# Small score pieces of two groups in one tile: windowed attention beside linear attention on one core

## The chip, the cores and the metric

The kernel runs on one core of a Trainium2 chip. That core has a matrix engine (PE in the profile, with its weight loads shown as PEld), a vector engine (DVE), a scalar engine (ACT), a general engine (POOL) and an engine that issues DMAs (SP). They run side by side and wait for each other through semaphores. The metric is the device time of one execution in microseconds (us), as a median of runs.

## The reference

Two attention blocks, A and B, each have an input of 2048 tokens x 640, weights of 640 x 1920 for queries, keys and values, and an output matrix of 640 x 640. There are 32 heads of 20 numbers each. The outputs of the two stand side by side.

```python
# A: sliding window of 256 keys
scores = jnp.einsum("bhqd,bhkd->bhqk", q, k) * (Dh ** -0.5)
mask = (idx[:, None] - idx[None, :] >= 0) & (idx[:, None] - idx[None, :] < W)
p = _softmax(jnp.where(mask[None, None], scores, -1e9), axis=-1)
o = jnp.einsum("bhqk,bhkd->bhqd", p, v)
return (lambda x, *d: x.transpose(*d))(o, 0, 2, 1, 3).reshape(B, S, D) @ wo
# B: linear attention
phi = lambda t: jnp.where(t > 0, t + 1, jnp.exp(t)) + 1e-6
kv = jnp.einsum("bhsd,bhse->bhde", phi(k), v)
den = jnp.einsum("bhqd,bhd->bhq", phi(q), z)[..., None] + 1e-6   # z: sum of phi(k)
o = jnp.einsum("bhqd,bhde->bhqe", phi(q), kv) / den
```

## The kernel before

**Segments, groups, pairs.** Tokens are cut into four segments of 512 (`SB`), s = 0 to 3. Heads are cut into eight groups of four (`NG`); groups are taken in pairs, g and h = g + 1. The four heads of a group lie in the four 32-row strips of PE's array, so that four matmuls with a depth of 20 can run beside each other.

**Pieces and tiles of scores.** For a segment and a group, the scores of the window are cut into pieces: blocks of 128 keys against a run of 64 to 256 queries (`first`, `before`, `last`), and a "middle" of four pieces of 64 queries (`M`). In a middle piece the upper 64 rows of the array's output are 64 keys of one block and the lower 64 rows are keys of the block two back, so that every one of its matmuls has 64 weight columns: the profile writes these 20*64, and the others 20*128. A tile holds 512 columns for each of four heads: it fills four PSUM banks, and there is one such tile in PSUM (`S_ps`), so a tile's scores can begin when the exponential of the tile before has read its own. `tiles_of` (L39) lists the tiles: for a pair in segment 0 four tiles, and else five, 76 in all.

**What happens to a tile.** `scores` (L752) writes the matmuls (L762), then one exponential on ACT over the whole tile (L780), which writes the tile `p` in SBUF, and then POOL sets to zero what lies outside the window, with `affine_select` (L794). A select of kind D or E (the diagonal and the window's far edge) works on 128 columns of each head, in place. A middle has two selects of 256 columns of each head: the first copies into a tile of its own, `plow`, what the own block keeps, and the second works in place on `p` for the far block.

**Values.** When a group has all its tiles, `values` (L805) is due two units later (`LAG = 2`): its matmuls (L821, 128*32: 128 keys, 32 output rows for each head) run over the group's pieces in the order of its tiles, four heads for each piece, 40 matmuls in segment 0 and 56 in the others. They read `p`, or `plow` for a middle's own block. DVE then transposes the result and divides it.

**The order.** A loop over the 76 tiles (from L1082) writes one unit for each: the scores of a tile, then the values of a group that is due, then as much filling work as the unit has credit for (`take`, L1067). Filling work is all else that PE does: projections of both blocks, the sums and outputs of B, the output projections. It comes from a plan with times (`plan`), in an order written ahead; every engine carries out its own instructions in that order. Filling work in the main loop evacuates PSUM with ACT or DVE, whichever has less load by the kernel's own account (`evac`).

**The start.** The first 512 tokens of A's x are loaded as they lie, in two halves (L172), and turned on PE (`transposes`, L178, with copies on DVE and ACT, L184 and L186). The weights of v come in two parts (L948), the first with `K0` of five blocks of 128 rows. `v_abreast` (L437) runs four chains of v's products beside each other in four PSUM banks: first all products whose weights are in the first part, then, chain by chain, the rest, with an evacuation after each. Then the second half of x is turned, and the other four chains of v follow. The weights of q and k are regrouped on three engines (L350 to L356), and their first chains precede the loop.

Of the kernel before, what the change touches and what calls it, by code (L numbers as in the profile page):

```python
# [9 lines left out]
P = 128  # L10
# [3 lines left out]
BF16 = mybir.dt.bfloat16  # L14
# [6 lines left out]
SB = 512  # L21
TPS = SB // P
# [10 lines left out]


HALF = P // 2
LOW = 2 * P


def tiles_of(s):  # L39

    def first(g):
        return [(g, 0, 64, 256, 0, P), (g, 1, 192, 256, HALF, P)], [("D", 0, P), ("E", SB - P, P)]

    def before(g, c):
        return [(g, -1, 0, 192, c, HALF), (g, -2, 0, 64, c + 192, HALF)], [("E", c + P, P)]

    def last(g, c):
        return [(g, 3, 448, 64, c, HALF), (g, 2, 320, 192, c + 64, HALF)], [("D", c, P)]

    def middle(g):  # L60
        return [(g, "M", P * i, HALF, LOW + HALF * i, HALF) for i in range(TPS)], [("M", LOW, LOW)]

    def tile_of(done, *pieces):
        return s, sum((p for p, _ in pieces), []), sum((q for _, q in pieces), []), done

    out = []
    for g in range(0, NG, 2):
        h = g + 1
        if s == 0:
            for gi in (g, h):  # L70
                out += [tile_of(None, first(gi)), tile_of(gi, last(gi, 0), middle(gi))]
            continue
        out += [
            tile_of(None, first(g)),
            tile_of(None, before(g, 0), middle(g)),
            tile_of(g, last(g, 0), middle(h)),
            tile_of(None, first(h)),
            tile_of(h, before(h, 0), last(h, 2 * P)),
        ]
    return out  # L80

# [11 lines left out]
def kernel(  # L93
# [11 lines left out]
    _, S, D = A_x.shape  # L105
# [9 lines left out]
    def pool(name, bufs, space=None):  # L115
        if space is None:
            return ctx.enter_context(tc.tile_pool(name=name, bufs=bufs))
        return ctx.enter_context(tc.tile_pool(name=name, bufs=bufs, space=space))
# [6 lines left out]
    pp = pool("p", 5)  # L125
    pqp = pool("pq", 2)
    op1 = pool("o1", 2)
    pl_ = pool("plow", 2)
    np_ = pool("norm", 1)
    tp = pool("turned", 1)  # L130
    rp = pool("rows", 2)
# [33 lines left out]
    def load_x_first():  # L165

        tok = pqp.tile([P, TPS, D], BF16, name="phi")
        src = xsrc["A"][0:SB, :].rearrange("(t p) d -> p t d", p=P)
        t = xp.tile([P, KT, SB], BF16, name="xA")

        def load(i):
            nc.sync.dma_start(out=tok[:, 2 * i : 2 * i + 2, :], in_=src[:, 2 * i : 2 * i + 2, :])  # L172

        def transposes(i):
            for tb in (2 * i, 2 * i + 1):
                ps = dps.tile([P, 2 * SB], BF16, name="dense")
                for c in range(KT):
                    nc.tensor.transpose(  # L178
                        ps[:, c * P : (c + 1) * P], tok[:, tb, c * P : (c + 1) * P], ident[:]
                    )  # L180
                dst = t[:, :, tb * P : (tb + 1) * P]
                pv = ps[:, 0:D].rearrange("p (c q) -> p c q", q=P)
                if tb % 2:
                    nc.scalar.activation(out=dst, in_=pv, func=ACT.Copy)  # L184
                else:
                    nc.vector.tensor_copy(out=dst, in_=pv)  # L186

        return t, load, transposes
# [67 lines left out]
    def evac(dst, src, n=SB, to=None):  # L256

        if to is None:
            to = "A" if load["A"] < load["D"] + AHEAD else "D"
        load[to] += n + COPY  # L260
        if to == "A":
            nc.scalar.activation(out=dst, in_=src, func=ACT.Copy)
        else:
            nc.vector.tensor_copy(out=dst, in_=src)

    def bank(wide=False):
        flush(begun[0] - 2)
        begun[0] += 1
        settle(False)
        if wide:  # L270
            return dps.tile([P, 2 * SB], BF16, name="dense")
        return dps.tile([P, SB], F32, name="dense")
# [40 lines left out]
    xA, xB = {}, {}  # L313
    q_pad, k_pad, v_tok = {}, {}, {}
# [6 lines left out]
    pieces = []  # L321
    for c in range(KT):
        m = EXTRA * c
        while m < EXTRA * (c + 1):
            n = min(EXTRA * (c + 1) - m, DH - m % DH)
# [83 lines left out]
    by_tokens = [(tb, i) for tb in range(TPS) for i in range(2)]  # L409
# [10 lines left out]
    def v_rows(ps, dst, tb, i):  # L420
        evac(
            dst[:, tb, i * hh : (i + 1) * hh, 0:DH],
            ps[:, 0 : hh * DH].rearrange("p (h d) -> p h d", d=DH),
            hh * DH,
        )
# [11 lines left out]
    def v_abreast(xt, dst, order, k0):  # L437
        pss = [bank() for _ in order]
        for ps, (tb, i) in zip(pss, order):
            for kt in range(k0):  # L440
                v_product(ps, xt, tb, i, kt)
        for ps, (tb, i) in zip(pss, order):
            for kt in range(k0, KT):
                v_product(ps, xt, tb, i, kt)
            v_rows(ps, dst, tb, i)

# [303 lines left out]
    def scores(s, parts, selects):  # L752
        S_ps = sps.tile([P, 4, SB], F32, name="S_ps")
        p_all = pp.tile([P, 4 * SB + 2], BF16, name="p")
        p = p_all[:, 0 : 4 * SB].rearrange("p (j q) -> p j q", j=4)
        nc.scalar.activation(out=p_all[0:1, 4 * SB : 4 * SB + 1], in_=ident[0:1, 0:1], func=ACT.Copy)

        def product(g, kb, k0, k1, q0, n, col, step):
            kt = k_pad[kb // TPS]
            ko = (kb % TPS) * P  # L760
            for j in range(4):
                nc.tensor.matmul(  # L762
                    columns(S_ps[k0:k1], j, col, n, step),
                    lhsT=kt[32 * j : 32 * j + DH, g, ko + k0 : ko + k1],
                    rhs=q_pad[s][32 * j : 32 * j + DH, g, q0 : q0 + n],
                    start=True,
                    stop=True,
                    tile_position=(32 * j, k0),
                )

        for g, rel, q0, n, col, step in parts:
            if rel == "M":
                own = key(s, q0 // P)
                product(g, own, 0, HALF, q0, n, col, step)

                far = own - 2 if own >= 2 else own
                product(g, far, HALF, P, q0 + (HALF if own >= 2 else 0), n, col, step)
            else:
                product(g, key(s, rel), 0, P, q0, n, col, step)
        nc.scalar.activation(out=p, in_=S_ps[:], func=ACT.Exp, scale=scale)  # L780
        add_load(a=2080)
        low = None
        if any(kind == "M" for kind, _, _ in selects):
            low = pl_.tile([P, 4, LOW], BF16, name="plow")
        for kind, c0, n in selects:

            v = p[:, :, c0 : c0 + n].rearrange("p j (b q) -> p j b q", q=HALF)
            if kind == "M":
                lv = low[:, :, c0 - LOW : c0 - LOW + n].rearrange("p j (b q) -> p j b q", q=HALF)
                jobs = [(lv, v, 1, 0), (v, v, -1, -HALF - 1)]  # L790
            else:
                jobs = [(v, v, 1, HALF) if kind == "D" else (v, v, -1, -1)]
            for dst, src, sgn, base in jobs:
                nc.gpsimd.affine_select(  # L794
                    out=dst,
                    in_=src,
                    pattern=[[0, 4], [0, n // HALF], [sgn, HALF]],
                    compare_op=ALU.is_ge,
                    fill=0.0,
                    base=base,  # L800
                    channel_multiplier=-sgn,
                )
        return p, low

    def values(s, g, held):  # L805
# [3 lines left out]
        todo = []  # L809
        for (_, rel, q0, n, col, step), (p, low) in held:  # L810
            if rel == "M":
                own = key(s, q0 // P)
                todo.append((own, low, q0, n, col - LOW, step))
                if own >= 2:
                    todo.append((own - 2, p, q0 + HALF, n, col, step))
            else:
                todo.append((key(s, rel), p, q0, n, col, step))
# [123 lines left out]

    xA[0], load_half, transposes = load_x_first()

    K0 = 2
    wv = A_wqkv.rearrange("(kt p) n -> p kt n", p=P)
    load_half(0)
    for k0, k1 in ((0, K0), (K0, KT)):
        nc.sync.dma_start(out=w_sb["A"][:, k0:k1, :], in_=wv[:, k0:k1, 2 * D : 3 * D])  # L948
# [4 lines left out]
    xB[0] = load_x("B", 0)  # L953
    dummies = warm_up((28, 3))
    next(dummies)
    transposes(0)
    next(dummies)
    v_tok[0] = v_bufs[0]
    v_abreast(xA[0], v_tok[0], by_tokens[0:4], K0)
    transposes(1)  # L960
    a_v0 = v_proj(xA[0], v_tok[0], by_tokens[4:])
    run(banks(a_v0, 2))
    regroup(0, raw[0], dve_copy, in_turn(act_copy, pool_copy))
# [118 lines left out]
    for i, (s, parts, selects, done) in enumerate(units):  # L1082
        p = scores(s, parts, selects)
# [6 lines left out]
        if ready and ready[0][0] + LAG <= i:  # L1090
            last = i == len(units) - 1
            if last:
                credit -= take(2000)
            _, at = ready.popleft()
# [10 lines left out]
    while ready:  # L1105
        take(5500)
        _, at = ready.popleft()
# [36 lines left out]
```

## Time and profile before

| what | before |
|---|---|
| median of 3 runs | 261.02 us (260.02 to 261.86) |
| profiled execution, its own time | 261.33 us |
| span of the profiled execution | 259.6 us |
| PE busy | 247.7 us, 95% |
| ACT, DVE, POOL busy | 200.3, 177.0, 171.8 us |
| exponentials of tiles (L780) | 76, 1.87 us each |
| selects of 512 elements, of 1024 into `p`, of 1024 into `plow` (L794) | 120, 32, 32; 0.71, 1.26, 1.21 us each |
| granted PE clock | 1.00 |

The span runs from the first to the last instruction of one execution; the time beside it is the device's own for the same execution. A row of the profile names a line, an engine, an operation, what it writes and reads, and the shape. "Busy" of PE is modelled: matmuls overlap, so a row's busy time is a union and not a sum of lengths. In a timeline, a row has its start and its length in us, and xN says that N instructions of one kind were drawn together; in square brackets are the idle time of the engine ahead of it and what ended it.

### The profile page before, as it was taken

The numbers are of one execution on the slowest core, as the hardware profiler recorded it, in microseconds if no ns is written. First come the engines' busy times: TensorE is split into PE (matmuls) and PEld (weight loads), VectorE is DVE, ScalarE is ACT, GpSimd is POOL, SyncE is SP. The second block draws the span as 40 slices with busy tenths as digits, with TensorE's granted clock in tenths as the row PEclk, the third lists the DMA queues.
The fourth block names the chain that finished last, engine by engine and source line by source line (L and its number), as shares of the span: only waits on it lengthen the run. The fifth ranks groups of instructions, "written<-read, shape, count | busy, mean of one in ns | idle before, by whom it ended". The sixth has DMA issues, their size and how long they took to land.

```text
span 259.6 us, 10761 instructions
## 1 busy us (share of the span) xinstructions
PE 247.7 (95%) x4722; PEld 142.4 (55%) x4769; DVE 177.0 (68%) x308; ACT 200.3 (77%) x260; POOL 171.8 (66%) x211
## 2 busy tenths in 40 slices
PE   8699999999999999999999999999999999999995
PEld 7444445556445745555456555555456554555573
DVE  0245686786745456866655578599889879978662
ACT  3376887899776788988676788888879998988742
POOL 6113777777696766759485796949767594976800
PEclk9999999999999999999999999999999999999999
DMA  6996579699568993502484591622857286975725
GB/s 186 312 231 182 79 198 136 103 279 216 92 95 247 114 257 88 163 3 48 84 132 122 58 190 43 170 43 59 173 89 174 48 188 168 109 136 120 233 47 186
DMA packets 65012, 36.35 MB, mean 140 GB/s; under 512 B 48197, under 2 KB 63941, under 8 KB 64965
## 3 DMA queue, kind: packets, MB, share of 16 engines
q1 hardware_dynamic: 64965, 35.67, 64.6%
q8 instruction: 37, 0.61, 1.0%
q14 instruction: 10, 0.08, 0.1%
HBM read 14.42 MB, written 9.83 MB: 93 GB/s over the span
## 4 chain that ended last, share of the span: by engine, by line
PE 80%; POOL 6%; issue 4%; ACT 3%; DVE 3%; DMA 3%; SPq 0%; ACTq 0%; DVEq 0%
PE dense L277 43%; PE S_ps L762 10%; PE dense L545 9%; PE dense L821 8%; PE dense L412 7%; POOL p L794 4%; DMA wA<-in_A_wqkv_dram 3%; ACT p L780 2%; POOL plow L794 2%; PE dense L652 1%; PE dense L695 1%; DVE phi L294 1%; ACT e L287 1%; PE dense L624 1%; DVE e L291 1%
## 5 line engine op out<-in xcount | busy, mean ns | idle before, releaser
L780 ACT ACTIVATE p<-S_ps 128x2048 bf16<-128x2048 f32 x76 | 142.4, 1873 | 33.9 <-PE S_ps L762 33.1
L794 POOL TENSOR_SCALAR_AFFINE_SELECT p<-p 128x512 bf16<-128x512 bf16 (+1 forms) x152 | 123.3, 822 | 63.8 <-ACT p L780 58.5
L277 PE MATMUL dense<-xA,wqk 128*128 128x512 bf16 x183 | 47.2, 379 | 1.1 <-issue 0.6
L794 POOL TENSOR_SCALAR_AFFINE_SELECT plow<-p 128x1024 bf16<-128x1024 bf16 x32 | 38.8, 1211 | 2.2
L762 PE MATMUL S_ps<-qpad,kpad 20*64 20x64 bf16 (+3 forms) x1728 | 35.2, 213 | 0.4
L762 PEld LDWEIGHTS <-kpad 20*64 20x64 bf16 (+1 forms) x1728 | 17.4, 100 | 30.0 <-issue 25.5
L834 DVE STREAM_TRANSPOSE T<-dense 128x512 f32<-128x512 f32 x32 | 22.8, 712 | 12.6 <-PE dense L821 12.5
L277 PEld LDWEIGHTS <-wqk 128*128 128x128 bf16 x200 | 18.5, 98 | 20.6 <-issue 1.3
L412 PE MATMUL dense<-wA,xA 128*128 128x320 bf16 x160 | 27.7, 300 | 2.1 <-DMA wA<-in_A_wqkv_dram 1.8
L291 DVE TENSOR_SCALAR e<-e 128x512 bf16<-128x512 bf16 x40 | 22.0, 550 | 10.7 <-ACT e L287 10.1
L294 DVE SCALAR_TENSOR_TENSOR phi<-dense,e 128x512 bf16<-128x512 f32 x40 | 27.7, 692 | 1.5
L821 PE MATMUL dense<-p,vA 128*32 128x64 bf16 (+2 forms) x1152 | 27.1, 223 | 0.5 <-POOL p L794 0.5
L277 PE MATMUL dense<-wB,xB 128*128 128x128 bf16 (+1 forms) x156 | 25.4, 297 | 0.8 <-issue 0.6
L287 ACT ACTIVATE e<-dense 128x512 bf16<-128x512 f32 x40 | 23.4, 594 | 2.5 <-PE dense L277 2.2
L277 PE MATMUL dense<-wo,oT 128*128 128x128 bf16 (+2 forms) x154 | 24.3, 296 | 1.0 <-issue 0.6
L545 PE MATMUL dense<-phi,tok 128*128 128x128 bf16 (+1 forms) x154 | 24.3, 296 | 0.7 <-issue 0.3
L277 PE MATMUL dense<-xB,wB 128*128 128x512 bf16 x90 | 24.2, 380 | 0.6 <-issue 0.3
L821 PEld LDWEIGHTS <-vA 128*32 128x32 bf16 x1664 | 22.2, 96 | 3.5 <-issue 1.4
L277 PE MATMUL dense<-wB,xA 128*128 128x512 bf16 (+1 forms) x156 | 23.4, 297 | 0.5 <-issue 0.3
L851 DVE TENSOR_TENSOR N<-T,recA 128x320 bf16<-128x320 f32 (+1 forms) x28 | 18.7, 668 | 3.1 <-DMA oT<-N 2.2
L412 PEld LDWEIGHTS <-xA 128*128 128x128 bf16 x160 | 14.3, 98 | 11.2 <-issue 3.1
L731 DVE TENSOR_TENSOR tok<-tok,rden 128x640 bf16<-128x640 bf16 x16 | 19.8, 1238 | 0.0
(68 smaller groups left out, 237.7 us busy)
## 6 DMA issues: line engine op xcount, KB each, us to landing
out_dram<-osb SPq DMA_DIRECT2D x7, 640.0 KB
x_scr<-xB SPq DMA_DIRECT2D x4, 640.0 KB
tok<-in_B_x_dram SPq DMA_DIRECT2D x4, 640.0 KB
xB<-x_scr SPq DMA_DIRECT2D x4, 640.0 KB
wB<-in_B_wqkv_dram SPq DMA_DIRECT2D x3, 800.0 KB
q_scr<-qpad SPq DMA_DIRECT2D x16, 60.0 KB
k_scr<-kpad SPq DMA_DIRECT2D x16, 60.0 KB
qpad<-q_scr SPq DMA_DIRECT2D x16, 60.0 KB
```

The lines of the kernel that those rows point to most:

```text
L277: nc.tensor.matmul(dst, lhsT=lhs(kt), rhs=rhs(kt), start=(kt == 0), stop=(kt == KT - 1))
L287: nc.scalar.activation(out=view(e), in_=src, func=ACT.Exp)
L291: nc.vector.tensor_scalar(out=e[:], in0=e[:], scalar1=1e-6, scalar2=1.0 + 1e-6, op0=ALU.add, op1=ALU.min)
L294: nc.vector.scalar_tensor_tensor(out=dst, in0=src, scalar=0.0, in1=view(e), op0=ALU.max, op1=ALU.add)
L412: nc.tensor.matmul(ps[:, 0 : hh * DH], lhsT=xt[:, kt, tb * P : (tb + 1) * P], rhs=w_sb["A"][:, kt, i * hh * DH : (i + 1) * hh * DH], start ...
L545: nc.tensor.matmul(out, lhsT=lhs(x, pk)[:, tb, :], rhs=rhs(pk, tb), start=(i == 0), stop=(i == len(blocks) - 1),)
L731: nc.vector.tensor_tensor(out=vh, in0=vh, in1=rden_of[s][:, tb, :, :].to_broadcast([P, H, DH]), op=ALU.mult)
L762: nc.tensor.matmul(columns(S_ps[k0:k1], j, col, n, step), lhsT=kt[32 * j : 32 * j + DH, g, ko + k0 : ko + k1], rhs=q_pad[s][32 * j : 32 * ...
L780: nc.scalar.activation(out=p, in_=S_ps[:], func=ACT.Exp, scale=scale)
L794: nc.gpsimd.affine_select(out=dst, in_=src, pattern=[[0, 4], [0, n // HALF], [sgn, HALF]], compare_op=ALU.is_ge, fill=0.0, base=base, chan ...
L821: nc.tensor.matmul(O_ps[32 * j : 32 * (j + 1), q0 : q0 + n], lhsT=v_flat[kb // TPS % 3][:, at + j * HV : at + j * HV + 32], rhs=columns(p, ...
L834: nc.vector.transpose(out=T.rearrange("p b e -> p (b e)"), in_=O_ps[:])
```

## The change

Two things are changed. In `tiles_of`, the middles of g and h share a tile, which holds nothing else; `last` (or, in segment 0, `last` of both groups) goes to a tile with other wide pieces. The number of tiles is the same. In segment 0, g is complete with the third tile of its pair and no longer with the second. `plow` has 512 columns in one buffer instead of 256 in two. At the start, the first part of v's weights has three blocks and the second has two, and the third and fourth turn of x stand behind the third and fourth chain of `v_abreast`, which is now a generator. Lines behind `tiles_of` move down by 5 to 7: scores L768, exponential L786, select L800, values L827.

```diff
-LOW = 2 * P
...
-    def middle(g):
-        return [(g, "M", P * i, HALF, LOW + HALF * i, HALF) for i in range(TPS)], [("M", LOW, LOW)]
+    def middle(g, c):
+        pieces = [(g, "M", P * i, HALF, c + HALF * i, HALF) for i in range(TPS)]
+        return pieces, [("M", c, TPS * HALF)]
...
+        w = 2 * P
         if s == 0:
-            for gi in (g, h):
-                out += [tile_of(None, first(gi)), tile_of(gi, last(gi, 0), middle(gi))]
+            out += [
+                tile_of(None, first(g)),
+                tile_of(None, last(g, 0), last(h, w)),
+                tile_of(g, middle(g, 0), middle(h, w)),
+                tile_of(h, first(h)),
+            ]
             continue
         out += [
             tile_of(None, first(g)),
-            tile_of(None, before(g, 0), middle(g)),
-            tile_of(g, last(g, 0), middle(h)),
+            tile_of(None, before(g, 0), last(g, w)),
+            tile_of(g, middle(g, 0), middle(h, w)),
             tile_of(None, first(h)),
-            tile_of(h, before(h, 0), last(h, 2 * P)),
+            tile_of(h, before(h, 0), last(h, w)),
         ]
...
-    pl_ = pool("plow", 2)
+    pl_ = pool("plow", 1)
...
-        def transposes(i):
-            for tb in (2 * i, 2 * i + 1):
+        def transposes(*tbs):
+            for tb in tbs:
...
             for kt in range(k0, KT):
                 v_product(ps, xt, tb, i, kt)
             v_rows(ps, dst, tb, i)
+            yield
...
-            low = pl_.tile([P, 4, LOW], BF16, name="plow")
+            low = pl_.tile([P, 4, SB], BF16, name="plow")
...
-                lv = low[:, :, c0 - LOW : c0 - LOW + n].rearrange("p j (b q) -> p j b q", q=HALF)
+                lv = low[:, :, c0 : c0 + n].rearrange("p j (b q) -> p j b q", q=HALF)
...
-    K0 = 2
+    K0 = 3
...
-    transposes(0)
+    transposes(0, 1)
     next(dummies)
     v_tok[0] = v_bufs[0]
-    v_abreast(xA[0], v_tok[0], by_tokens[0:4], K0)
-    transposes(1)
+    for i, _ in enumerate(v_abreast(xA[0], v_tok[0], by_tokens[0:4], K0)):
+        if i > 1:
+            transposes(i)
```

More of the change, by code (lines that the diff above doesn't have):

```diff
@@ L812, in values @@
                 own = key(s, q0 // P)
-                todo.append((own, low, q0, n, col - LOW, step))
+                todo.append((own, low, q0, n, col, step))
                 if own >= 2:
```

## The prediction

> **What bounds the kernel now.** I read the page's first part first, then the timeline of one group pair, then the waits of PE.
>
> ```profile
> PE 247.7 (95%) x4722; PEld 142.4 (55%) x4769; DVE 177.0 (68%) x308; ACT 200.3 (77%) x260; POOL 171.8 (66%) x211
> ```
>
> PE is busy 95% of 259.6 us. Of the 11.9 us that are left, most lie ahead of 8.5 us and at the end. Between 19.4 and 242 us PE is busy 217.0 of 222.6 us, and the longest wait in that stretch is 0.3 us. So, whatever shortens PE's instruction stream there shortens the kernel, and whatever makes PE wait lengthens it, one for one. The timeline of 98 to 108 us shows a period of the loop (start, length, engine, line):
>
> ```profile
> 101.30 0.55 PE L762 MATMUL S_ps<-qpad,kpad 20*128 20x64 bf16 x40
> ...
> 101.78 0.82 PE L277 MATMUL dense<-wB,xB 128*128 128x512 bf16 x3
> ...
> 102.03 1.88 ACT L780 ACTIVATE p<-S_ps 128x2048 bf16<-128x2048 f32 x1 [0.37 <-PE S_ps L762]
> ...
> 104.34 0.40 PE L762 MATMUL S_ps<-qpad,kpad 20*128 20x256 bf16 x8
> ...
> 104.67 0.56 PE L277 MATMUL dense<-wB,xB 128*128 128x128 bf16 x7
> ...
> 107.33 0.40 PE L762 MATMUL S_ps<-qpad,kpad 20*128 20x192 bf16 x16
> ...
> 107.66 0.52 PE L821 MATMUL dense<-p,vA 128*32 128x256 bf16 x16
> ```
>
> The reader sees three score phases. From a phase's first matmul to the next other one it is 0.48 us with 40 matmuls (8 wide pieces in the 20*128 form, 32 small ones in 20*64), 0.33 us with 8 and 0.33 us with 16, all of the 20*128 form. The tile of 101.30 completes group g; the values of g start 6.36 us later, at 107.66, two units on.
>
> **What the change removes: array forms.** In a 40-phase the start times of single matmuls put the first small one at 0.221 us, the last at 0.360 and what follows at 0.481. The 64 + 192 columns ahead take about 0.11 us (two such pairs fill 0.15 us of a 16-phase and then leave), so about 0.11 us is the change of form. Each pair of groups, in all four segments, has two 40-phases now; after the change one becomes a 16-phase (0.33) and the other a phase of 64 small matmuls, which no row shows. Its bounds: 0.33 us, no better than a wide phase, and 0.66 us (the 1024 small ones are busy 10.6 us, so 64 x 10.4 ns). I take 0.40: two stretches of 0.14 us and the 0.12 us of leaving, the row of start times being nearest. Entering the small form straight from 128*128 is not shown either; entering the 20*128 form puts 0.10 us on a 512-column matmul (0.31 from start to start, against 0.22), and I take the same, between 0 and the 0.11 of the inner change. Saved: 0.96 - 0.33 - 0.40 = 0.23 us a pair, x 16 pairs = **3.7 us** (-0.5 to 4.8). All of it is on PE's path. The number of tiles (76) and exponentials, and the columns of filling work in each unit, stay (segment 0's move by a unit).
>
> **What it moves: POOL's selects.** Now a tile has at most three selects, D (512 elements) and the two of M (1024), and there are two such tiles for each pair. After, the small tile has four 1024-element selects in a row and the others two of 512. The source view of the select between 70 and 160 us has min/median/max:
>
> ```profile
> L794 POOL TENSOR_SCALAR_AFFINE_SELECT p<-p x61: 667/667/1154, 69.6 to 157.6; 128x512 bf16<-128x512 bf16 x49, 128x1024 bf16<-128x1024 bf16 x12
> L794 POOL TENSOR_SCALAR_AFFINE_SELECT plow<-p x12: 1153/1154/1319, 72.4 to 149.3; 128x1024 bf16<-128x1024 bf16 x12
> ```
>
> POOL's total doesn't change (4 x 1.15 a pair either way), but its end after the exponential does: from 0.07 + 0.67 + 2 x 1.15 + 0.14 = 3.2 us to 0.07 + 4 x 1.15 + 3 x 0.07 = 4.9 us. That matters if the values of g wait for the last of the four, though it belongs to group h. The trace of before shows that such a wait exists. PE's timeline of 211.5 to 213.5 us, and POOL's of 211 to 212:
>
> ```profile
> 212.37 0.21 PE L821 MATMUL dense<-plow,vA 128*32 128x64 bf16 x4
> 212.40 0.23 PE L821 MATMUL dense<-p,vA 128*32 128x64 bf16 x5
> 212.89 0.29 PE L821 MATMUL dense<-p,vA 128*32 128x64 bf16 x7 [0.27 <-POOL p L794]
> ```
> ```profile
> 211.23 1.61 POOL L794 TENSOR_SCALAR_AFFINE_SELECT p<-p 128x1024 bf16<-128x1024 bf16 x1
> ```
>
> These are the values of the group whose last tile was the one of 205.5 us. The 49th matmul, head 0 of a piece that only D touches, ran; the 50th, head 1 of the same piece, waited until 212.89, right behind the select that ended at 212.84, which is h's upper M on other columns of the same p. So, heads 1 to 3 wait for every in-place select of a tile. In the order of the changed program the same wait stands at the 30th of g's matmuls (40 or 56), the first that reads head 1 from the small tile's p, and counts that tile's fourth select. Nothing of g in before stands so: there, h's M came third, and g's reading of that tile came at the 49th.
>
> The race, counted from the small tile's first score matmul, in the middle stage:
> - p is ready at 0.65 (the 0.73 from 101.30 to 102.03, less the shorter phase) + 1.88 exponential + 4.88 (above) + 0.05 wake-up = 7.46 us.
> - PE arrives at 6.36 - 0.08 (the shorter phase) + 0.49 (place of the 30th matmul) = 6.77 us.
> - PE waits **0.69 us**.
>
> The selects aren't always at the minimum: over the run they average (40.3 + 38.8) us / 64 = 1.24 us, which gives 1.05; to the middle I allot 0.75. In the last quarter a select beside an L731 takes 1.61 us as above; with one of four so, the wait is 1.15. Segment 0 has the same two full units between (3.03 us each, from 36.90 to 39.92 and so on) and comes to 0.74. In the last pair PE arrives 1.0 us later (values at 243.25, tile at 235.86), so its wait is about 0.1. Sum: 11 x 0.75 + 4 x 1.15 + 0.1 = **13.0 us**. Ends: 0 if the wait isn't there, and 1.61 for two of every four selects, 15 x 1.6 = 24 us.
>
> Behind the waiting matmul stand the rest of the values, 1.5 us of filling work (3584 columns) and the next score phase, so nothing fills the gap, and DVE's transposition of the values waits with it. The next score phase is not late a second time: its exponential ended 0.4 us ahead now, and more after.
>
> [...]
>
> With the new order the small waits of this kind in before (0.06, 0.36 and 0.28 us net at 167, 212 and 228 us) are replaced: -0.7 us.
>
> Also moved: plow goes from two buffers of 256 columns to one of 512. The small tile's first select then waits for the values of the h before, which stand one unit ahead (unit 6 of a pair, its reuse in unit 7, about 3 us); it costs nothing unless POOL were that early.
>
> **The start.** PE's timeline of 3 to 12 us:
>
> ```profile
> 5.35 1.40 PE L412 MATMUL dense<-wA,xA 128*128 128x320 bf16 x8
> 8.54 1.79 PE L412 MATMUL dense<-wA,xA 128*128 128x320 bf16 x12 [1.80 <-DMA wA<-in_A_wqkv_dram]
> 10.17 0.72 PE L178 MATMUL dense<-ident,phi 128*128 128x128 bf16 x10
> 11.20 0.99 PE L412 MATMUL dense<-wA,xA 128*128 128x320 bf16 x6 [0.31 <-DVE xA L186]
> ```
>
> The first weights (320 KB) landed at 5.11, the rest (480 KB) at 8.50, the second half of x at 9.39. With 480 KB ahead, the first part lands near 5.11 + 160/480 x 3.39 = 6.2; 12 products end by 8.3 (12 x 0.175), still ahead of 8.50. Then 8 products remain instead of 12: 4 x 0.149 = 0.6 us less, and the turn's copies (0.31 us wait) hide behind the fourth chain. The turn adds nothing to PE; it waits for the first chains' evacuations (0.44 us on ACT), and x has landed by then. SP issues the same DMAs in the same order. What is late next is the regrouped weights: k's load lands at 13.87, and its chains came at 17.2. **-0.7 us** (0 to -1.0; +0.5 if the first part lands near 7.5).
>
> **The sum.** The profiled execution took 261.33 us (259.6 span + 1.7 around it), 0.3 above the median. 261.3 - 3.7 - 0.7 - 0.7 + 13.0 = 269.2, and 0.3 less on the median's scale: **269.0 us**.
>
> **Rivals.**
> - *The wait isn't there or is covered* (the other side): if the values of g need only g's selects, p is ready 2.4 us earlier and PE never waits; it decides from 0.69 us on. 261.0 - 3.7 - 0.7 - 0.7 = 256. For it: PE waited for POOL 0.5 us in all so far. Against: the 50th matmul at 212.89. Chance 0.07.
> - *Half of the wait*: PE comes later by 0.3 us a pair, since DVE or ACT hold up filling work. 15 x 0.4 = 6; 262. Chance 0.06.
> - *No gain from the forms*: the 64-phase runs at 0.66 us. 269.0 + 4.2 = 273. Chance 0.12.
> - *Longer selects*: two of four take 1.61 everywhere, as L731's neighbours do in the last quarter (205.5 us: 1.28, 1.61, 1.15, 1.61). 269 + 11 = 280. Chance 0.06. [...]
>
> The forecast itself has 0.69. A change under 1% (2.6 us) can't be told from none here. The range leaves out the first and the last rival and most of the second: **264.5 to 275**. Faster by over 1%: 0.07; within: 0.06; slower: 0.87.
>
> **What would show it.** Right: PE idle at the values line (L827 after) with POOL as releaser, 0.5 to 1.3 us in each of some 15 pairs; two kinds of score phase at 0.33 us and one near 0.40; first score phase at 18.7 us. Wrong: no such idle time (then 256), or POOL selects well over 1.2 us on average.

## The result and the profile after

The changed kernel takes **269.03 us** (median; 268.55 to 270.32) against 261.05 us of the kernel before: a ratio of 1.032, with a 95% interval of 1.029 to 1.035. The forecast was 269.0 us. The sum came out; two of its four terms did not, and it is luck that their errors nearly cancelled. The profiled execution took 268.69 us with a span of 267.0 us, 7.4 us above the span of before. That is less than the 8 us between the medians: the starts of these two executions lie further apart than the start is worth, as shown below.

The page of the changed kernel, part 1 and the first line of the chain (part 4), and the same line of the chain before:

```profile
PE 248.4 (93%) x4717; PEld 145.4 (54%) x4769; DVE 173.5 (65%) x306; ACT 202.2 (76%) x262; POOL 171.1 (64%) x211
...
PE 42%; POOL 31%; ACT 12%; issue 9%; DVE 2%; DMA 2%; SPq 0%; POOLq 0%; ACTq 0%
```
```profile
PE 80%; POOL 6%; issue 4%; ACT 3%; DVE 3%; DMA 3%; SPq 0%; ACTq 0%; DVEq 0%
```

PE's busy time is what it was, 248 us, in a longer span. In before PE had 80% of the chain that ended last and POOL 6%; now POOL has 31% and ACT 12%. POOL is no busier (171.1 us for 171.8): it is on the path because somebody waits for it. Who does is one line of PE's waits (us in total, times, longest), after and before:

```profile
PE dense L827 <- POOL p L800: 8.0, 15, 1.2
```
```profile
PE dense L821 <- POOL p L794: 0.5, 2, 0.3
```

One pair in PE's and POOL's timelines, the one whose small tile starts at 102.81 us:

```profile
102.81 0.70 PE L768 MATMUL S_ps<-qpad,kpad 20*64 20x64 bf16 x64
...
103.58 1.88 ACT L786 ACTIVATE p<-S_ps 128x2048 bf16<-128x2048 f32 x1 [0.41 <-PE S_ps L768]
...
108.99 0.40 PE L768 MATMUL S_ps<-qpad,kpad 20*128 20x192 bf16 x16
...
109.33 0.63 PE L827 MATMUL dense<-p,vA 128*32 128x256 bf16 x24
...
109.78 0.20 PE L827 MATMUL dense<-plow,vA 128*32 128x64 bf16 x4
109.81 0.19 PE L827 MATMUL dense<-p,vA 128*32 128x64 bf16 x1
110.40 0.21 PE L827 MATMUL dense<-p,vA 128*32 128x64 bf16 x3 [0.40 <-POOL p L800]
```
```profile
105.53 1.15 POOL L800 TENSOR_SCALAR_AFFINE_SELECT plow<-p 128x1024 bf16<-128x1024 bf16 x1 [1.33 <-ACT p L786]
106.75 1.15 POOL L800 TENSOR_SCALAR_AFFINE_SELECT p<-p 128x1024 bf16<-128x1024 bf16 x1
107.97 1.15 POOL L800 TENSOR_SCALAR_AFFINE_SELECT plow<-p 128x1024 bf16<-128x1024 bf16 x1
109.19 1.82 POOL L800 TENSOR_SCALAR_AFFINE_SELECT p<-p 128x1024 bf16<-128x1024 bf16 x2
```

Of the values, 24 + 4 + 1 = 29 matmuls run; the 30th comes at 110.40. In the last row two selects are drawn together, and the first of them is the small tile's fourth: 109.19 + 1.15 = 110.34, 0.06 us ahead of the 30th matmul. The profile counts 0.40 us as idle, since it models a matmul as running for 0.19 us; from start to start the gap is 0.59 us. Over the 16 pairs these gaps sum to 11.1 us: 0.54 to 0.73 in 12 pairs, 0.98, 1.05 and 1.40 in the three whose values start at 186, 217 and 233 us, 0.24 in the last pair.

The same trace shows the small phase: 102.81 to 103.45 (the first weight load of the filling work), 0.64 us and not 0.40. Where the time of a pair went, from score phase to score phase, in the middle of the run: the unit with the new wide tile 0.19 us shorter (0.15 of it in the phase), the small one 0.16 longer, the unit of g's values longer by the wait, the others as before.

### The profile page after: what moved, and what is told of

Read it like the earlier page. It is cut to its first block, busy times and chain, and to the rows that moved or that the text cites. A ratio compares the mean times of both kernels' runs of the same rounds, so it can differ in the third digit from the quotient of the medians.

```text
span 267.0 us, 10758 instructions
## 1 busy us (share of the span) xinstructions
PE 248.4 (93%) x4717; PEld 145.4 (54%) x4769; DVE 173.5 (65%) x306; ACT 202.2 (76%) x262; POOL 171.1 (64%) x211
## 4 chain that ended last, share of the span: by engine, by line
PE 42%; POOL 31%; ACT 12%; issue 9%; DVE 2%; DMA 2%; SPq 0%; POOLq 0%; ACTq 0%
PE dense L282 23%; POOL p L800 18%; POOL plow L800 13%; ACT p L786 11%; PE dense L417 5%; PE S_ps L768 5%; PE dense L551 4%; PE dense L827 3%; DMA wA<-in_A_wqkv_dram 2%; DVE e L296 1%; ACT osb L267 1%; PE dense L701 1%; POOL kv_T L606 0%; PE dense L894 0%; ACT p L762 0%
## 5 line engine op out<-in xcount | busy, mean ns | idle before, releaser
L786 ACT ACTIVATE p<-S_ps 128x2048 bf16<-128x2048 f32 x76 | 142.4, 1874 | 35.1 <-PE S_ps L768 33.9
L800 POOL TENSOR_SCALAR_AFFINE_SELECT p<-p 128x512 bf16<-128x512 bf16 (+1 forms) x152 | 122.4, 815 | 53.6 <-ACT p L786 47.4
L800 POOL TENSOR_SCALAR_AFFINE_SELECT plow<-p 128x1024 bf16<-128x1024 bf16 x32 | 38.6, 1206 | 22.9 <-ACT p L786 20.1
L827 PE MATMUL dense<-p,vA 128*32 128x64 bf16 (+2 forms) x1152 | 29.0, 222 | 8.0 <-POOL p L800 8.0
L768 PE MATMUL S_ps<-qpad,kpad 20*64 20x64 bf16 (+3 forms) x1728 | 35.5, 217 | 0.3
L768 PEld LDWEIGHTS <-kpad 20*64 20x64 bf16 (+1 forms) x1728 | 19.7, 99 | 26.5 <-issue 25.0
L296 DVE TENSOR_SCALAR e<-e 128x512 bf16<-128x512 bf16 x40 | 23.1, 577 | 13.6 <-ACT e L292 13.1
L827 PEld LDWEIGHTS <-vA 128*32 128x32 bf16 x1664 | 22.4, 97 | 14.2 <-issue 11.1
L282 PE MATMUL dense<-wB,xB 128*128 128x512 bf16 (+1 forms) x153 | 25.2, 296 | 1.0 <-issue 0.6
L267 ACT ACTIVATE osb<-dense 128x512 bf16<-128x512 f32 (+1 forms) x25 | 13.9, 570 | 8.1 <-PE dense L282 6.8
L857 DVE TENSOR_TENSOR N<-T,recA 128x320 bf16<-128x320 f32 (+1 forms) x28 | 17.5, 623 | 1.0
```

The lines of the kernel that those rows point to most:

```text
L282: nc.tensor.matmul(dst, lhsT=lhs(kt), rhs=rhs(kt), start=(kt == 0), stop=(kt == KT - 1))
L296: nc.vector.tensor_scalar(out=e[:], in0=e[:], scalar1=1e-6, scalar2=1.0 + 1e-6, op0=ALU.add, op1=ALU.min)
L768: nc.tensor.matmul(columns(S_ps[k0:k1], j, col, n, step), lhsT=kt[32 * j : 32 * j + DH, g, ko + k0 : ko + k1], rhs=q_pad[s][32 * j : 32 * ...
L800: nc.gpsimd.affine_select(out=dst, in_=src, pattern=[[0, 4], [0, n // HALF], [sgn, HALF]], compare_op=ALU.is_ge, fill=0.0, base=base, chan ...
L827: nc.tensor.matmul(O_ps[32 * j : 32 * (j + 1), q0 : q0 + n], lhsT=v_flat[kb // TPS % 3][:, at + j * HV : at + j * HV + 32], rhs=columns(p, ...
L857: nc.vector.tensor_tensor(out=dst[:, :, at : at + b - a], in0=T[:, :, a - lo : b - lo], in1=r[:].to_broadcast([P, SB // 32, b - a]), op=AL ...
```

## The experiments

The first question is whether the wait is for selects that g doesn't need, or whether POOL's burst hurts by itself. The second is what the start and the tiles each give alone. The third is why the small phase takes 0.64 us. "Before" was 260.8 to 260.9 us in the runs beside these kernels.

**p as a tile of exactly 4 x 512.** The kernel has two spare columns at the end of each row of p, and plow has none. Reads of plow in the changed kernel don't wait for h's select: at 233.89 us they start while h's select into plow (232.43 to 234.04) still works. So the spare columns of p were taken away:

```diff
-        p_all = pp.tile([P, 4 * SB + 2], BF16, name="p")
-        p = p_all[:, 0 : 4 * SB].rearrange("p (j q) -> p j q", j=4)
-        nc.scalar.activation(out=p_all[0:1, 4 * SB : 4 * SB + 1], in_=ident[0:1, 0:1], func=ACT.Copy)
+        p = pp.tile([P, 4, SB], BF16, name="p")
+        nc.scalar.activation(out=p[0:1, 0, 0:1], in_=ident[0:1, 0:1], func=ACT.Copy)
```

> The changed kernel with one difference: p is a tile of exactly four heads x 512 columns (it had two columns more, for ScalarE's small copy ahead of the exponential, which now writes the first element that the exponential writes over). In the order of instructions the values of g then wait only for g's own two selects of the small tile, not for the fourth. Theory A (PE's wait is for h's selects on other columns of the same p): p is ready 0.77 + 1.88 + 0.07 + 2 x 1.15 + 0.07 + 0.05 = 5.1 us after the small tile's first score matmul, PE arrives at 7.0, so the 11.0 us of waits in the changed kernel's trace all go: 258.0 us, faster than before by about 1%. Rival B (POOL's burst of four selects itself holds up what follows, in whatever order it is read): PE waits at another place, at the tile behind or at the exponential, and the time stays above 265 us.

Measured: 258.64 us, ratio to before 0.993 (0.990 to 0.995), 0.6 us above theory A's time. In its timelines of PE and POOL:

```profile
107.78 0.63 PE L826 MATMUL dense<-p,vA 128*32 128x256 bf16 x24
108.24 0.20 PE L826 MATMUL dense<-plow,vA 128*32 128x64 bf16 x4
108.26 0.20 PE L826 MATMUL dense<-p,vA 128*32 128x64 bf16 x4
108.29 0.20 PE L826 MATMUL dense<-plow,vA 128*32 128x64 bf16 x4
```
```profile
104.05 1.15 POOL L799 TENSOR_SCALAR_AFFINE_SELECT plow<-p 128x1024 bf16<-128x1024 bf16 x1 [1.24 <-ACT p L785]
105.27 1.15 POOL L799 TENSOR_SCALAR_AFFINE_SELECT p<-p 128x1024 bf16<-128x1024 bf16 x1
106.37 1.15 POOL L799 TENSOR_SCALAR_AFFINE_SELECT plow<-p 128x1024 bf16<-128x1024 bf16 x1
107.59 1.81 POOL L799 TENSOR_SCALAR_AFFINE_SELECT p<-p 128x1024 bf16<-128x1024 bf16 x2
```

The values run past 108.26 while the fourth select (107.59 to 108.74) still works. POOL's burst is the same, and nobody waits for it: theory A, and B falls. Exponentials (1.88 us) and large selects (1.20 us on average, for 1.19) are as long as with the spare columns. The 10.4 us between 269.0 and 258.6 are the price of the wait, and this kernel is faster than both, by 0.7% than before.

**POOL's fourth select done twice.** The output is the same.

```diff
                 jobs = [(lv, v, 1, 0), (v, v, -1, -HALF - 1)]
+                if c0:
+                    jobs.append(jobs[1])
```

> The changed kernel with POOL's fourth select of each small tile done twice (the second changes nothing). If PE's wait in the values of g is for the last select of the tile, each of the 16 pairs waits 1.15 + 0.07 us more: 269.0 + 16 x 1.22 = 288.5 us, and the waits in the trace go from 11.0 to about 30 us. If the wait is set by something that ends at the same time (the exponential of the tile behind, the transposition of the values on DVE), the time stays within 2 us of 269.

Measured: 294.59 us (292.26 to 299.53), ratio 1.127 (1.119 to 1.136). The line of PE's waits, and the clock's row on the page:

```profile
PE dense L829 <- POOL p L802: 28.2, 16, 2.6
```
```profile
PEclk9999997999999999799996999989799999979999
```

All 16 pairs wait, and the gaps at the 30th matmul sum to 31.3 us, 20.1 more than in the changed kernel: 1.26 a pair for a select of 1.15 + 0.07. The wait follows the last select, nearly one for one. The time rose by 25.6 us and not by 19.5, and the second row says why: the granted clock fell to half for 3.4 us at five places and for 6.8 us at one, 23.9 us in all in the profiled execution (299.53 us), which is worth up to 12 us. At one of them, from 120.81 us, five matmuls of 512 columns take 2.05 us, and the five from 106.68 take 1.24. All four executions have a mean clock below one, 0.960 to 0.988. An estimate, each time less its span times the missing share of the clock, gives 287.4 to 288.8 us, where 288.5 was expected. The profiled execution of the changed kernel, whose waits reach 1.4 us, kept the clock at 1.00, and so did four of its other five; the sixth had 0.992.

**The start alone, and the tiles alone.** The first is the kernel before with the edits of `transposes`, `v_abreast` and `K0` from the change; the second is the change without them.

> The kernel before with the second change alone: first weights of v 3 to 2, the third and fourth turn of x between v's chains. The prediction's sum had -0.7 us for it, 260.3; the trace of the changed kernel has its first score phase 1.77 us earlier (17.65 for 19.42), which would make 259.3. If the extra 1.1 us is a faster load in that one execution (300 KB in a us for 230 between 4.5 and 7 us), the time is 260.3 and the trace's second part of the weights lands near 8.5 us again; if the order of the loads gives it, 259.3 and it lands near 7 us.

> The changed kernel with the old start: the new tiles alone. The start alone measured 0.75 us below before, so the tiles alone should measure 269.0 + 0.75 = 269.8 us, 9.0 us over before. If the start's gain in the changed kernel's profiled execution (1.8 us) were the rule, it would be 270.8.

Measured: the start alone 260.03 us, ratio 0.997 (0.996 to 0.999), 0.75 us better than the before beside it; the tiles alone 269.92 us, ratio 1.037 (1.034 to 1.041). The two add up: 261.0 - 0.75 + 9.06 = 269.3. Both expectations' first numbers hold to 0.3 us. The start of the changed kernel and of the start alone, in PE's timelines:

```profile
5.75 2.60 PE L417 MATMUL dense<-wA,xA 128*128 128x320 bf16 x18 [0.16 <-DMA wA<-in_A_wqkv_dram]
8.40 0.44 PE L183 MATMUL dense<-ident,phi 128*128 128x128 bf16 x5
8.68 0.43 PE L417 MATMUL dense<-wA,xA 128*128 128x320 bf16 x2
8.95 0.44 PE L183 MATMUL dense<-ident,phi 128*128 128x128 bf16 x5
9.43 2.89 PE L417 MATMUL dense<-wA,xA 128*128 128x320 bf16 x20
```
```profile
6.56 2.60 PE L412 MATMUL dense<-wA,xA 128*128 128x320 bf16 x18 [1.50 <-DMA wA<-in_A_wqkv_dram]
9.21 0.44 PE L178 MATMUL dense<-ident,phi 128*128 128x128 bf16 x5
```

In both the wait between the two parts is gone, and the turns stand between the chains without a gap. But the same loads land at different times: the first 480 KB at 5.71 in the one and 6.52 in the other, at 5.24 in the kernel with exact p, where the second part came at 8.53 and PE waited 1.50 us for it; over seven traces with the new start the first score phase lies between 17.5 and 18.8 us (five of them up to 17.8), over three with the old one between 18.5 and 19.5. So two profiles do not tell the worth of the start: the 1.8 us between the traces of the changed kernel and of before were 0.75 by the timed runs. The loads' spread from execution to execution is not explained here.

**The exact p in the kernel before, and with the new start.** The first is the edit of p above, on the kernel before; the second adds the new start. Both keep the old tiles.

> The kernel before with the exact p alone. The few waits of PE for h's selects (0.06, 0.36 and 0.28 us at 167, 212 and 228 us) go, and nothing else moves: 260.3 us, 0.7 below before. If the two columns matter in another way too (another layout of p in its reads or writes), the exponential or the selects change their length, and the time moves by more than 2 us.

> The kernel before with the new start and the exact p, but the old tiles. By the phase lengths in the two traces (0.48 + 0.48 us a pair before, 0.33 + 0.64 after) the new tiles gain nothing by themselves but 0.04 us a pair in the values of h: 261.05 - 0.7 - 1.8 = 258.6 us, within 0.6 us of the changed kernel with exact p (258.0). If the array forms are worth the 3.7 us of the prediction, that one is faster by 3 us or more than this one.

Measured: 260.03 us, ratio 0.998 (0.996 to 1.000), and 259.38 us, ratio 0.995 (0.993 to 0.997). The wait was worth 0.75 us in before, 0.7 expected (the interval just reaches to no change). With exact p and the new start on both sides, the new tiles stand at 258.64 against 259.38: they are worth 0.7 us, far from the prediction's 3.7, and the intervals of the two ratios overlap (0.990 to 0.995 and 0.993 to 0.997), so that no more than a small gain can be claimed. The traces point the same way: from the first score phase to the last it takes 221.5 us with the old tiles and 220.8 in the kernel with pieces in turn, below, which has the new ones.

**Why the small phase takes 0.64 us.** The start times of its single matmuls, in ns behind the first, in the changed kernel at 87.52 us (the k-th of 64):

```
k        1   2   3  ...   31   32    33    34    35  ...   63   64   next
start    0   3   6  ...  135  139   238   246   255  ...  488  496    638
```

The first 32 come 4.5 ns apart on average, as the 32 of a 40-phase did; then there is a step of 99 ns, and the rest come 8.3 ns apart. The 33rd is also the first that belongs to h. Two edits on the kernel with exact p tell the two apart. The first writes the pieces in turn from g and h:

```diff
+        if parts[0][1] == "M":
+            parts = [x for two in zip(parts[:TPS], parts[TPS:]) for x in two]
```

> The changed kernel with exact p; the eight small pieces of the small tile are written in turn from g and h, not g's four and then h's four. In the changed kernel the first 32 matmuls of the small phase start 4.5 ns apart, the 33rd 99 ns later, and the rest 8.3 ns apart, so that the phase takes 0.64 us. Theory S (the instructions ahead of the phase are ready in a store of 64, and those behind come at 8.3 ns a pair of weight load and matmul): the step stays at the 33rd and the phase at 0.64. Rival G (the 33rd is h's first, and going to another group's keys and queries costs it): the step goes, or stands at the 9th, and the phase is 0.40 or well over 0.7. Time within 0.6 us of 258.6 by theory S.

Measured: 258.88 us, ratio 0.993 (0.990 to 0.995). The step stands at the 33rd, 139 to 238, and the phase takes 0.638 us, though groups now change every eight matmuls: not the group. The second puts one chain of filling work between the halves:

```diff
-        for g, rel, q0, n, col, step in parts:
+        for i, (g, rel, q0, n, col, step) in enumerate(parts):
+            if rel == "M" and i == TPS:
+                lent.append(take(5 * SB))
...
+    lent = []
...
         credit += rate
+        if lent:
+            credit -= lent.pop()
```

> The changed kernel with exact p; one chain of filling work (up to 5 x 512 columns, taken from the unit's credit) stands between g's 32 small score matmuls and h's 32. By theory S each half then runs from the store, 0.14 us for its starts and 0.12 to leave, with no step, and the two take 0.52 us and one more change of form (about 0.1): the time stays at 258.6, within 0.6. If h's half is slow for what it does (its columns 256 to 511 of the banks, its keys), it stays at 8.3 ns a matmul.

Measured: 271.63 us, ratio 1.042 (1.039 to 1.045). Both halves run as theory S has it: 32 starts in 139 ns, 0.26 us each, h's like g's. The time was missed by 13 us, for a reason of its own. PE's waits and its timeline:

```profile
PE S_ps L767 <- ACT p L787: 10.6, 16, 0.9
```
```profile
88.04 0.33 PE L767 MATMUL S_ps<-qpad,kpad 20*64 20x64 bf16 x32
...
89.59 0.33 PE L767 MATMUL S_ps<-qpad,kpad 20*64 20x64 bf16 x32
...
92.09 0.40 PE L767 MATMUL S_ps<-qpad,kpad 20*128 20x256 bf16 x8 [0.85 <-ACT p L787]
```

The exponential can start only behind the second half, at 90.16, and ends at 92.04; the filling work lent to the gap is missing behind it, and PE stands until S_ps is free. That is 10.6 of the 13 us; the rest was not taken apart. Behind the second half, which ended at 89.86, PE thus needed 2.2 us of other work, and a unit without values has about 2.6 us of filling (6144 columns): little to lend.

So the slow half is a matter of how many matmuls stand in a row, and not of group or column. A reading that fits, an estimate from these start times, is that the phase is bound by the supply of instructions: the 64 ahead of the step, 32 weight loads and 32 matmuls, are ready when PE turns to it, and those behind come at 4.2 ns each, half of 8.3. The trace of before has the same rate in another array form: behind its 40-phase of 98.36 us, 26 weight loads in a row for the values of h (128*32) come 8.3 ns apart, while in the kernel with exact p, behind the 16-phase of 113.23 us, no more than seven do. So the rate stood in the trace before the change, and the prediction did not use it. That a store of instructions is behind the step was not shown by itself.

## Why the prediction was right, step by step

- **What bounds the kernel** held: PE's order of work. Waits put into it came out in the time: 10.4 us for the false wait by the exact p, 9.06 for the new tiles with their wait. PE's idle time before was not mostly at the two ends, as the prediction reads it: 5.6 of the 11.9 us lie between 19.4 and 242 us, in pieces of at most 0.3 us. The sum doesn't use that.
- **The wait at the 30th matmul** held in place, releaser and recurrence: 15 waits by the profile, 16 gaps by start times. Nothing filled the gaps: between 109.81 and 110.40 us no matmul starts, though filling work stands next behind the values. Its size was put at 13.0 us; it measured 11.1 by the gaps of one trace and 10.4 by the timed runs. The step that failed is the small tile's phase: with 0.64 us instead of 0.40, p is ready 0.12 us later than reckoned (7.59 for 7.46), but PE also comes 0.23 us later (7.0 for 6.77). So a middle pair waits 0.59 and not 0.69, and the allotted 0.75 was high, as the selects stayed at 1.15 there.
- **The array forms** were mis-sized: "I take 0.40 ... the row of start times being nearest" failed. The start times of 32 matmuls were doubled, and the second 32 don't come at the rate of the first. The other bound, 0.66, from the busy time of the 1024 small matmuls, came close, but by luck: that time is modelled, and for each 40-phase it has 0.14 us of starts and one matmul's 0.19, and no slow second half. The rival with a chance of 0.12, no gain from the forms, is what happened: phases of 0.97 us a pair for 0.96. What is left is 0.04 us a pair in the values of h, whose last matmul starts 0.62 us behind the first after a 16-phase and 0.66 after a 40-phase. Over 16 pairs that is 0.6 us, about the 0.7 of the runs. That four matmuls with a depth of 20 run beside each other shows in before's phase of 104.34 us: four of 256 columns start within 10 ns, the other four at 119 to 130 ns.
- **The start** was put at -0.7 and measured -0.75 by the timed runs. The sign given for it, a first score phase at 18.7 us, was not what the changed kernel's trace shows (17.65).
- **The old waits** were put at -0.7 and measured -0.75.
- So 3.0 us too much gain from the forms stood against 2.6 us too much wait (13.0 against 10.4), and that the sum came closer than its parts is luck. (The recorded terms add up to 268.9 rather than 269.0.)
- **The rivals.** That the wait isn't there was priced at 256; the kernel in which it isn't there takes 258.6, by the missing gain of the forms. PE did come later than reckoned, as in the rival of half the wait, but by the small phase, which delays p too. Longer selects happened late in the run alone: five of the 64 large ones took over 1.2 us (1.48 to 1.84), all behind 184 us and beside L737, which is L731's new line, and four of them stand ahead of the waits of 0.98, 1.05 and 1.40 us. The 64 average 1.19 us, for 1.24 before, so a burst did not meet such an instruction everywhere.

## What to carry to other kernels

The likely reading of the false wait is that a semaphore wait covers what the tool that orders the instructions takes to overlap, which can be more than what is read. Here two spare columns in a row made reads of one group wait for writes to another's columns, which cost 0.75 us as long as those writes came early and 10 us when they came last. So look, before work is gathered into one tile, at which write each reader really counts, and check whether a plain layout takes the wait away. And don't extend the rate of a short burst: 32 small matmuls at 4.5 ns say nothing of the next 32 (8.3 ns here, behind a step of 99). Look in the old trace for a longer row of small instructions, in whatever form.

## What the runs showed of the hardware that was not expected

- In the changed kernel's small phase of 87.52 us, pairs of a small weight load and a matmul start 4.5 ns apart on average for 32 pairs, then after a step of 99 ns every 8.3 ns.
- In the kernel with the fifth select, PE has a gap of 1.75 to 2.75 us about every 17 us, and the granted clock fell to half six times in the profiled execution, for 3.4 us or twice that, each time within 1.8 us behind such a gap; ten of the 16 gaps were not followed by a fall. In the profiled execution of the changed kernel, with gaps of up to 1.4 us, it never fell. That the gaps are the cause is the author's estimate from these times and not shown: the kernel with the broken phase, whose waits are at most 0.9 us by the profile, had one such fall (a mean clock of 0.994), and single executions of the changed kernel (0.992), of the tiles alone and of before with exact p (0.993 each) had a lower clock too, which stays open.
- The same first loads land up to 1.3 us apart from execution to execution (the first 480 KB at 5.24 us with exact p, at 6.52 with the start alone).
